# Holding back loads of x and of Q's weights behind the first statistics in a fused attention and feed-forward kernel

## The chip, the cores and the metric

One core of a Trainium2 chip. The metric is the device time of one execution in microseconds (us), the median of several. All runs here are in the fast state; the executions of one kernel can spread by 2 us and more. Two sources of that spread are found below: the grid of TensorE's clock (e5), and a pause worth 0.4 us that comes and goes.

Names: PE is TensorE (matmuls), PEld its weight loads, DVE is VectorE, ACT is ScalarE, POOL is GpSimd, SP is SyncE, which here only issues DMAs.

## The reference

```python
xn = layernorm(x)                                   # x: 2048 x 576, bf16
q, k, v = split(xn @ wqkv)                          # 32 heads of 18
pq, pk = phi(q), phi(k)                             # phi(t) = t+1 if t>0 else exp(t)
attn = ((pq @ (pk.T @ v)) / (pq @ sum(pk))) @ wo    # linear attention, per head
ffn  = (gelu(xn @ w_gate) * (xn @ w_up)) @ w_down   # 576 -> 4608 -> 576
out  = x + attn + ffn
```

## The kernel before

The part that matters is the start. x comes in 16 tiles of 128 rows. SyncE issues its loads, ScalarE's queue issues K's weights; each weight matrix is one load of 512 rows and one of 64 rows (Q's has a third, a copy of the last 64).

```python
def load_x(n0, cnt):
    nc.sync.dma_start(x_sb[:, n0:n0 + cnt, :], x_view[:, n0:n0 + cnt, :])

# ... tile pools, buffers
def load_w(which, on=nc.sync):
    c = slice(which * D, (which + 1) * D)
    on.dma_start(wqkv_sb[:, 0:4, c], A_wqkv[0:512, c].rearrange("(kt p) c -> p kt c", p=P))
    on.dma_start(wqkv_sb[0:HP, 4, c], A_wqkv[512:576, c])
    if which == 0:
        on.dma_start(wq_lo[HP:P, :], A_wqkv[512:576, c])

nc.scalar.preload_act_table_set("natural_log_exp_and_others")
load_x(0, 1)
load_x(1, 1)
load_x(2, 2)
load_x(4, 4)
load_w(0)                      # Q's weights
load_x(8, 4)
load_x(12, 4)
nc.vector.memset(wqkv_sb[HP:P, 4, :], 0.0)
nc.vector.memset(wqkv_sb[0:1, 0, D:D + 2], 0.0)
load_w(1, nc.scalar)           # K's weights
# ... identity, small constants
spin(NWARM)                    # 38 matmuls on the identity, to bring TensorE's clock up
```

Then a list `todo` of (time, step, tile), sorted by time, gives each engine its order: the statistics of a tile (`ln_stats`, DVE), its normalisation, its transposes, the K matmuls (`k_half`, two of five matmuls each), phi, and so on. Ten more warming matmuls stand in it at 5.80, 6.20 and 8.50.

```python
todo += [(t, spin, count) for t, count in [(5.80, 3), (6.20, 5), (8.50, 2)]]
todo.sort(key=lambda x: x[0])
```

Of the kernel before, what the change touches and what calls it, by code (L numbers as in the profile page):

```python
# [56 lines left out]
def kernel(  # L57
# [11 lines left out]
    nc = tc.nc  # L69
# [20 lines left out]
    x_sb = persist.tile([P, NS, D], BF16, name="x_sb")  # L90

    def load_x(n0, cnt):
        nc.sync.dma_start(x_sb[:, n0:n0 + cnt, :], x_view[:, n0:n0 + cnt, :])
# [13 lines left out]
# [6 lines that stand above are left out]
# [2 lines left out]
    load_x(0, 1)  # L115
    load_x(1, 1)
    load_x(2, 2)
    load_x(4, 4)
    load_w(0)
    load_x(8, 4)  # L120
    load_x(12, 4)

    nc.vector.memset(wqkv_sb[HP:P, 4, :], 0.0)
    nc.vector.memset(wqkv_sb[0:1, 0, D:D + 2], 0.0)
# [393 lines left out]
    def timed(steps, count):  # L518
        for step, times in steps:
            last = len(times) - 1  # L520
            for n in range(count if last >= 4 else last + 1):
                if times[min(n, last)] is not None:
                    yield times[min(n, last)] + TILE * max(n - last, 0), step, n

    todo = [*timed(STEPS, NS), *timed(Q_STEPS, NQ)]
# [6 lines left out]
        ]  # L532

    todo += [(t, spin, count) for t, count in [(5.80, 3), (6.20, 5), (8.50, 2)]]
    todo.sort(key=lambda x: x[0])

    tail = next(i for i, (_, step, n) in enumerate(todo) if step is STEPS[-1][0] and n == NS - 1) + 1
# [203 lines left out]
```

## Time and profile before

| | before |
|---|---|
| time, median (beside the changed kernel) | 527.63 us, 527.35 to 527.99 |
| span of the profiled execution | 525.2 us |
| K's large load, issued to landed | 1.95 to 9.59 us |
| TensorE's wait for it | 3.12 us |
| granted clock of TensorE over the span | 0.996 |

The time line shows the wait and the issues before it. Its columns are start, length, engine and line, operation, output and input, count, and in brackets the idle time before and what ended it.

```profile
0.81 1.82 SPq L93 DMA_DIRECT2D x_sb<-in_A_x_dram  x4
2.67 0.43 SPq L109 DMA_DIRECT2D wqkv_sb<-in_A_wqkv_dram  x1
9.63 1.36 PE L249 MATMUL ps_all<-wqkv_sb,xnT 128*128 128x288 bf16 x5 [3.12 <-DMA wqkv_sb<-in_A_wqkv_dram]
```

The reader is to see that SyncE issues four loads of x without a pause, Q's weights right behind them at 2.67, and that the first K matmuls come only at 9.63.

### The profile page before, as it was taken

To read this page: it belongs to the slowest core of one execution; us is meant where nothing else is said; L and a number is where in the kernel's file an instruction comes from. 1 tells how busy PE (TensorE), PEld (TensorE's weight loads), DVE (VectorE), ACT (ScalarE), POOL (GpSimd) and SP (SyncE) were. 2 spreads that over 40 slices of the span, in tenths; PEclk is the share of its full clock that TensorE was granted. 3 is DMA by queue.
4 is the path that set the end of the run, shared out by engine and by line. 5 is a ranking of instruction groups with operands and counts; after the bars stand their busy time and mean duration, and the time that the engine had idled before them with its cause. 6 is when DMAs were issued, how large, how long until landed. Compare 5 with 4: busy or idle time off the path is not lost.

```text
span 525.2 us, 10640 instructions
## 1 busy us (share of the span) xinstructions
PE 517.4 (99%) x4498; PEld 314.8 (60%) x4498; DVE 250.9 (48%) x435; ACT 143.2 (27%) x293; POOL 35.2 (7%) x55
## 2 busy tenths in 40 slices
PE   6999999999999999999999999999999999999997
PEld 5777764555577754444577744444777544445775
DVE  5997564987348513333378133334485233333101
ACT  3998543223230013232200023233000122322000
POOL 2021100112002100000011000000021000000000
PEclk8999999999999999999999999999999999999999
DMA  8233808899610035555400055555100355540000
GB/s 278 54 58 63 219 2 233 246 271 265 178 34 24 12 100 143 159 153 154 116 13 12 18 168 154 152 156 146 45 24 13 102 149 157 148 136 2 12 11 24
DMA packets 106282, 57.89 MB, mean 110 GB/s; under 512 B 13370, under 2 KB 105722, under 8 KB 106234
## 3 DMA queue, kind: packets, MB, share of 16 engines
q1 hardware_dynamic: 105626, 56.55, 38.3%
q8 instruction: 35, 0.57, 0.4%
q10 hardware_dynamic: 608, 0.66, 0.4%
q14 instruction: 13, 0.11, 0.1%
HBM read 52.86 MB, written 2.36 MB: 105 GB/s over the span
## 4 chain that ended last, share of the span: by engine, by line
PE 97%; DMA 2%; ACT 0%; DVE 0%; issue 0%
PE ps_all L317 55%; PE ps_all L677 27%; PE ps_all L249 4%; PE ps_all L682 4%; PE ps_all L293 4%; PE ps_all L346 2%; DMA wqkv_sb<-in_A_wqkv_dram 1%; DMA xnT<-xn 1%; PE ps_all L455 1%; PE ps_all L437 0%; PE ps_all L659 0%; ACT L114 0%; PE ps_all L235 0%; DVE res L685 0%; ACT phi_e L269 0%; PE ps_all L426 0%
## 5 line engine op out<-in xcount | busy, mean ns | idle before, releaser
L317 PE MATMUL ps_all<-xnT,wg 64*128 64x512 bf16 x1152 | 272.6, 376 | 0.0
L317 PE MATMUL ps_all<-xnT,wu 64*128 64x512 bf16 x1152 | 271.7, 376 | 0.0
L648 DVE TENSOR_TENSOR hT<-ps_all,gl 128x512 bf16<-128x512 f32 x144 | 99.5, 691 | 161.9 <-ACT gl L647 161.2
L647 ACT ACTIVATE gl<-ps_all 128x512 f32<-128x512 f32 x144 | 86.1, 598 | 314.3 <-PE ps_all L317 294.9
L317 PEld LDWEIGHTS <-wu 64*128 64x128 bf16 x1152 | 108.3, 94 | 66.3
L317 PEld LDWEIGHTS <-wg 64*128 64x128 bf16 x1152 | 108.3, 94 | 66.1
L677 PE MATMUL ps_all<-wd_sb,hT 128*128 128x288 bf16 x1152 | 147.0, 286 | 0.0
L677 PEld LDWEIGHTS <-hT 128*128 128x128 bf16 x1152 | 112.3, 98 | 30.6 <-issue 1.3
L479 DVE RECIPROCAL den_sb<-den_sb 126x128 f32<-126x128 f32 (+1 forms) x80 | 68.3, 911 | 0.5
L685 DVE TENSOR_TENSOR res<-ps_all,x_sb 128x288 bf16<-128x288 f32 x32 | 14.6, 458 | 88.0 <-PE ps_all L682 88.0
L317 PE MATMUL ps_all<-xnT,wr 64*128 64x512 bf16 x288 | 55.1, 376 | 0.0
L482 POOL TENSOR_TENSOR pqT<-pqT,den_sb 126x512 bf16<-126x512 bf16 (+3 forms) x25 | 24.2, 966 | 317.3 <-DVE den_sb L479 282.7
L249 PE MATMUL ps_all<-wqkv_sb,xnT 128*128 128x288 bf16 x160 | 23.6, 296 | 3.3 <-DMA wqkv_sb<-in_A_wqkv_dram 3.1
L682 PE MATMUL ps_all<-m_sb,pqT 126*128 126x288 bf16 (+1 forms) x160 | 24.9, 285 | 0.0
L317 PEld LDWEIGHTS <-wr 64*128 64x128 bf16 x288 | 14.5, 94 | 16.9 <-issue 0.7
L293 PE MATMUL ps_all<-hT,xn 128*128 128x288 bf16 (+4 forms) x176 | 22.4, 276 | 0.0
L249 PEld LDWEIGHTS <-xnT 128*128 128x128 bf16 x160 | 15.8, 100 | 9.6 <-issue 3.3
L293 PEld LDWEIGHTS <-xn 128*128 128x128 bf16 (+1 forms) x176 | 17.5, 101 | 4.1
L682 PEld LDWEIGHTS <-pqT 126*128 126x128 bf16 (+1 forms) x160 | 15.5, 97 | 4.1
L346 PE MATMUL ps_all<-xnT,wqkv_sb 128*126 128x512 bf16 (+1 forms) x70 | 17.4, 378 | 0.0
L277 DVE SCALAR_TENSOR_TENSOR hT<-ps_all,phi_e 128x288 bf16<-128x288 f32 x32 | 13.2, 449 | 8.1 <-ACT phi_e L273 7.5
L269 ACT ACTIVATE phi_e<-ps_all 128x288 f32<-128x288 f32 x32 | 12.9, 410 | 6.8 <-PE ps_all L249 5.5
(67 smaller groups left out, 175.3 us busy)
## 6 DMA issues: line engine op xcount, KB each, us to landing
wg<-in_B_w_gate_dram SPq DMA_DIRECT2D x72, 256.0 KB, 2.9
wu<-in_B_w_up_dram SPq DMA_DIRECT2D x72, 256.0 KB, 3.5
wd_sb<-in_B_w_down_dram SPq DMA_DIRECT2D x12, 432.0 KB, 4.5
wr<-in_B_w_gate_dram SPq DMA_DIRECT2D x72, 32.0 KB, 2.7
wr<-in_B_w_up_dram SPq DMA_DIRECT2D x72, 32.0 KB, 3.0
out_dram<-res SPq DMA_DIRECT2D x15, 144.0 KB, 1.8
x_sb<-in_A_x_dram SPq DMA_DIRECT2D x3, 576.0 KB, 8.0
wqkv_sb<-in_A_wqkv_dram SPq DMA_DIRECT2D x2, 576.0 KB, 4.5
```

The source lines that it names most:

```text
L249: nc.tensor.matmul(ps_all[:, k_bank(n, hf), :HALF], lhsT=xnT[:, kt, n * P:(n + 1) * P], rhs=wqkv_sb[:, kt, D + hf * HALF:D + (hf + 1) * HALF],
L277: nc.vector.scalar_tensor_tensor(out=out_, in0=ps, scalar=0.0, in1=e, op0=ALU.max, op1=ALU.add)
L293: nc.tensor.matmul(ps_all[:m, b, col:col + w], lhsT=xn[:, n, j0:j0 + m], rhs=pk[:, n, d0:d0 + w], start=(n == 0 and col == 0), stop=(n == ...
L317: return nc.tensor.matmul(self.outs[i], lhsT=self.lhs(i, rows, kt), rhs=self.rhs(i, rows, kt), start=start, stop=stop, skip_group_check=True,)
L346: nc.tensor.matmul(ps, lhsT=wqkv_sb[:, kt, q0:q0 + rows], rhs=xnT[:, kt, sc * SC:(sc + 1) * SC], start=(kt == 0), stop=(kt == KT - 1),)
L479: nc.vector.reciprocal(out=d[:, h:h + P], in_=d[:, h:h + P])
L482: nc.gpsimd.tensor_tensor(out=pqT[:rows, c, cols], in0=pqT[:rows, c, cols], in1=d, op=ALU.mult)
L647: nc.scalar.activation(out=gl[:], in_=ps_all[:, b[0], :], func=ACT.Gelu_apprx_tanh)
L648: nc.vector.tensor_tensor(out=hT[:, GUB * k + i, :], in0=ps_all[:, b[1], :], in1=gl[:], op=ALU.mult)
L677: nc.tensor.matmul(acc, lhsT=hT[:, f, j * P:(j + 1) * P], rhs=wd_sb[:, f, hs], start=(f == 0), stop=False,)
L682: nc.tensor.matmul(acc, lhsT=pqT[:rows, c, ts_], rhs=m_sb[:rows, c, hs], start=False, stop=(c == NCH - 1),)
L685: nc.vector.tensor_tensor(out=res[:, hs], in0=acc, in1=x_sb[:, n, hs], op=ALU.add)
```

## The change

The intent: x's tiles 4 to 15 and Q's weights aren't needed early, so they are issued only when the statistics of the first tile are done, and K's weights meet less traffic. The hold is a write of two elements into the place that the load of tile 4 will fill: the load has to wait for it, and the other loads follow in SyncE's order.

```diff
     load_x(2, 2)
-    load_x(4, 4)
-    load_w(0)
-    load_x(8, 4)
-    load_x(12, 4)
 ...
     todo += [(t, spin, count) for t, count in [(5.80, 3), (6.20, 5), (8.50, 2)]]
+
+    todo += [(4.0, lambda n: nc.vector.memset(x_sb[0:1, n, 0:2], 0.0), 4)]
+    todo += [(4.01, lambda n: load_x(n, 4), n) for n in (4,)]
+    todo += [(4.02, lambda n: load_w(0), 0)] + [(4.03, lambda n: load_x(n, 4), n) for n in (8, 12)]
```

## The prediction

> **What bounds the kernel now.** I read the page's chain first, then the waits of TensorE, then the first 16 us step by step. The chain that ended last, by engine:
>
> ```profile
> PE 97%; DMA 2%; ACT 0%; DVE 0%; issue 0%
> ```
>
> TensorE carries nearly everything. The waits of TensorE over the whole span are only three: 1.4 us at the very start, 3.1 us for a part of wqkv_sb, and 0.2 us for a transpose at 50.3 us. So the change, which touches only the first microseconds, can win at most what the 3.1 us wait holds, plus what that wait causes. The chain in order of time (start, length, what):
>
> ```profile
> 1.95 7.64 DMA wqkv_sb<-in_A_wqkv_dram
> 9.59 0.04 issue
> 9.63 1.36 PE ps_all L249 x5
> 10.99 0.53 PE ps_all L235 x5
> 11.52 1.20 PE ps_all L249 x5
> ...
> 14.96 0.28 PE ps_all L235 x5
> 15.24 0.62 PE ps_all L249 x5
> ```
>
> The load of K's weights, issued on ScalarE's queue at 1.95, lands at 9.59 and releases the first K matmuls (L249). The reader should also see that the same five matmuls take 1.36 us here and 0.62 us at 15.24, and five transposes (L235) 0.53 against 0.28. The reason is in the table of windows (stretch, its length, then busy time of PE, PEld, DVE, ACT, POOL, the granted TensorE clock, DMA share, GB/s):
>
> ```profile
> 5.79:9.20 3.41, 0.72 (x12) 0.64 (x11) 2.55 (x9) 0.98 (x3) 0.63 (x3) 1.00 1.06 353
> 9.20:12.61 3.41, 2.98 (x16) 2.10 (x16) 0.00 (x0) 1.46 (x4) 0.00 (x0) 0.50 1.05 322
> 12.62:16.00 3.38, 3.38 (x36) 2.83 (x35) 3.18 (x10) 3.32 (x12) 0.24 (x1) 1.00 0.25 98
> ```
>
> While TensorE waited (busy 0.72 of 3.41 us), the clock went to half at 9.20 and came back 3.41 us later. The clock records put the edges at 5.79, 9.20 and 12.62, on one grid of 3.413 us.
>
> Why is the load so slow? The queues in three stretches, 3.5 to 5.25, 5.25 to 7 and 7 to 9.6 us (q1 is SyncE's queue, q10 ScalarE's; packets, MB, share):
>
> ```profile
> q1 hardware_dynamic: 156, 0.42, 61.3%
> q10 hardware_dynamic: 115, 0.13, 22.7%
> ...
> q1 hardware_dynamic: 134, 0.43, 64.4%
> q10 hardware_dynamic: 203, 0.23, 37.5%
> ...
> q1 hardware_dynamic: 513, 0.58, 75.6%
> q10 hardware_dynamic: 290, 0.30, 34.7%
> ```
>
> The DMA engines are full throughout, and K's 0.66 MB get only a third of the 2.09 MB moved. The q1 bytes beside them are the end of x's tiles 2 and 3 (0.18 MB), x's tiles 4 to 7 (0.59) and most of Q's weights (0.66). For comparison, V's weights, a load of the same shape issued at 50.22 when the queues are empty, needs:
>
> ```profile
> DMA to landing us min/median/max: 4.5/4.5/4.5
> ```
>
> [...]
>
> **The change part by part.** It removes nothing from the work: the same loads with the same bytes. It adds a two-element write by VectorE into x's tile 4, after the first statistics. I compared the instruction order: it is in VectorE's stream right behind the first aggregate, and SyncE's load of tiles 4 to 7 waits for it; Q's weights and the two later x loads follow in SyncE's order. No other wait changes.
>
> - *The added write.* The aggregate runs 3.94 to 4.15 us; a small write of this kind took 0.06 us (three of them at 1.86 to 1.88). VectorE's later work moves by at most 0.1 us, and TensorE waits for weights then anyway: worth 0.
> - *The hold.* The load of tiles 4 to 7 was issued at 2.20; now at about 4.2, as SyncE starts within about 0.05 us of its release. The hold is 2 us, not until K has landed. The first x load had its first packet 1.0 us after issue, V's weights 1.2 us: so x's 4608-byte packets come from about 5.2 to 5.45 on.
> - *K before, as a check of the method.* Per DMA engine K has 36 packets, tiles 2 and 3 have 5 left at 3.85 us, tiles 4 to 7 have 8. Taking turns: 5 x (93+51) ns = 0.72, then 8 x (178+51) ns = 1.83, then 23 x (51+51) ns = 2.35; the sum ends at 8.75. It landed at 9.59[...].
> - *K after.* 5 turns with tiles 2 and 3 to 4.57; then K alone until x4 comes at 5.2 to 5.45. At 51 to 65 ns a packet that is 10 to 17 packets, in all 15 to 22. V's load, however, ramps up slowly (43 packets over all engines in its first half microsecond, 126 after one, 274 after 1.5), so I take 13 to 20. 16 to 23 remain: 8 with x (1.83 us), 8 to 15 with Q (0.8 to 1.5). End 7.85 to 8.8, plus 0.84 (0.6 if the tail shrinks with it): landing 8.4 to 9.6, centre 8.7. [...] the floor is V's time, 1.95 + 4.48 = 6.4.
> - *TensorE.* Start moves from 9.63 to about 8.75, 0.9 us. If the clock still falls at 9.20, the part before 9.20 (0.45 us) is won in full and the part from 9.20 to 9.63 (0.43 us) at half, so 0.45 + 0.2 = 0.65 us. If TensorE's load in the window is enough to keep the clock, the cold stretch is won too: its chain 9.63 to 13.12 is 3.49 us, at full clock 0.62 + 0.28 + 0.62 + 0.11 + 0.28 = 1.91, so up to 1.6 more; ScalarE, 96% busy from 11 to 16 us, would hand back part, so I count 1.0 to 1.3.
> - *Later on.* Tiles 4 to 7 are first read at 13.39, Q's weights at 16.38; their landing moves from 7.99 to about 8.5 to 9, and from 11.8 to about 12, since the total of bytes is the same and the engines stay full. Neither reaches the path. From 16 us on the chain is TensorE without gaps, so a gain at the start arrives at the end.
>
> Sum: 0.65 at the centre with the fallen clock, 2 to 3 with the clock kept or an early landing, 0 at worst; weighted about 1.1 us of 527.37, thus 526.3.
>
> **The rivals.** (1) *The hold is too short and nothing is won*: x's large packets come back while half of K is outstanding and take 78% of each turn. For it: the arithmetic above. Against: the bytes ahead of K do fall. Time 527.0 to 527.4. (2) *K really has the engines to itself and lands near 6.7*, the clock never falls: 3 us of wait plus about 1.3 of cold clock, 523.0 to 523.5. For it: V's 4.5 us alone. Against: x4 comes back at 5.3, when even V's load would have been under half done. (3) *A new wait*: tile 4's statistics or Q's first unit wait for the held loads. It would need Q's weights 2 us later than I work out; then the gain is lost and the time is 527 to 529. (4) *Clock grid*: if it shifts between executions, the runs of one kernel would spread by about a microsecond; the three of before spread by 0.5.
>
> **Range and chances.** Everything lies within 1% of 527.37, since the whole wait and the cold clock are worth 4.7 us together; 2% would be 10.5 us. Range 523.9 to 527.4. Faster by over 2%: 0.01; within: 0.98; slower: 0.01.
>
> **What would show it.** In the changed profile: SyncE's fourth load is issued at about 4.2; q10 has moved over 0.2 MB by 5.3; K's weights land between 8.4 and 9; L249's first wait is near 2.2 us; the clock still halves at 9.2 and comes back at 12.6. Wrong would be: a landing before 7.5[...], or a wait of VectorE for x.

Passages for which no trace of this case stands are cut from it: a paragraph of general rules, what the 0.84 us was put down to (it is the landing at 9.59 less the sum's end at 8.75), a clause on a possible landing at 7.5 with its cause, and the causes beside two of the signs with one of these signs. The sum came to 0.65 us at the centre, 2 to 3 in the better cases and 0 at worst, weighted about 1.1 us of 527.37, thus 526.3. That the two queues take turns packet by packet is the author's assumption in this arithmetic, not a measurement (e5 and e7 give counts for it). Measured in the packet records of before are the medians of one packet (51 ns for 1152 bytes, 93 for 2304, 178 for 4608 bytes from 4.2 to 6.5 us) and counts: from 4.2 to 6.5 us 224 of K's 1152-byte packets started, and 160 of SyncE's queue (116 of 4608 bytes, 42 of 2304, 2 of 1152). Such counts don't give the order, since the records name no engine.

## The result

| | before | after |
|---|---|---|
| time, median of 4 | 527.63 us (527.35 to 527.99) | 523.53 us (523.40 to 523.66) |
| span of the profiled execution | 525.2 us | 521.7 us |
| K's large load lands | 9.59 us | 7.37 us |
| TensorE's wait for it | 3.12 us | 0.79 us |
| first Q matmul starts | 16.52 us | 13.48 us |
| granted clock over the span | 0.996 | 1.000 |

The ratio is 0.9922, with a 95% interval of 0.9905 to 0.9939. A ratio is the mean time of one kernel's fast runs over that of the other's of the same rounds, so not quite the ratio of the medians. The gain of 4.1 us is clear of noise, and 523.53 us lies below the predicted range of 523.9 to 527.4.

The chain of the kernel after, first by engine and then in order of time (start, length, what):

```profile
PE 97%; DMA 1%; ACT 1%; DVE 0%; issue 0%
```

```profile
1.95 5.42 DMA wqkv_sb<-in_A_wqkv_dram
7.37 0.04 issue
7.41 0.79 PE ps_all L245 x5
...
8.22 0.41 ACT phi_e L265
8.63 0.58 ACT xnT L234
...
12.04 0.77 PE ps_all L245 x5
```

K's load took 5.42 us in place of 7.64. Its five matmuls (L245 is the old L249, since line numbers moved by four) took 0.79 us in place of 1.36, so the clock was full (granted 1.00 from 4.60 to 8.01, below). And between 8.2 and 12.0 the chain now runs through ScalarE and VectorE, which in the kernel before waited for a slow TensorE (its chain there is TensorE alone from 9.63 to 16 us).

The time line of the kernel after:

```profile
4.14 0.06 DVE L532 MEMSET x_sb<- 1x1 uint32 x1
4.62 0.43 SPq L109 DMA_DIRECT2D wqkv_sb<-in_A_wqkv_dram  x1
7.41 0.77 PE L245 MATMUL ps_all<-wqkv_sb,xnT 128*128 128x288 bf16 x5 [0.79 <-DMA wqkv_sb<-in_A_wqkv_dram]
```

The added write cost 0.06 us. The load of tiles 4 to 7 was issued at 4.25, 0.05 us after the write's end, Q's weights at 4.62. The queues from 3.5 to 5.25 and from 5.25 to 7 us (packets, MB, share of the 16 engines; q10 carries K):

```profile
q10 hardware_dynamic: 307, 0.35, 62.4%
q1 hardware_dynamic: 102, 0.20, 31.0%
...
q1 hardware_dynamic: 67, 0.30, 58.4%
q10 hardware_dynamic: 301, 0.31, 52.4%
```

By 5.25 us K had moved 0.35 MB, where it had moved 0.13 before. The packet records say when x came back: its first 4608-byte packet started at 5.66 us, 1.4 us after its issue, when 444 of K's 608 packets had started (queue view, 3.5 to 5.65 us; 576 of the 608 carry data). The last K packet started at 6.88.

The windows of the kernel after (stretch, length, busy PE, PEld, DVE, ACT, POOL, clock, DMA share, GB/s):

```profile
4.60:8.01 3.41, 2.29 (x28) 1.71 (x27) 3.31 (x12) 1.64 (x6) 0.48 (x2) 1.00 1.05 344
```

The clock records of this execution have their first edge at 4.60 us, where that of before had one at 5.79. On a grid of 3.41 us the window around the wait therefore is 4.60 to 8.01; TensorE was busy for 2.29 us of it, and the clock stayed at 1.00.

**Where the time went**, profile against profile, 525.2 - 521.7 = 3.5 us. The first K matmul starts 9.63 - 7.41 = 2.2 us earlier. From it to the first Q matmul it takes 13.48 - 7.41 = 6.07 us in place of 16.52 - 9.63 = 6.89, another 0.8. The last 0.4 or so lies further on: from the first Q matmul to the end of the last matmul takes 505.7 us in before and 505.3 in after. In before TensorE is released late at 50.35 us (the chain there runs through a transpose). The same 505.7 stands in e2, e8, e11 and in e16, a later run of the very kernel after, and 505.3 stands in e1, e4 and e15, so I take this part for chance, not for the change. That the medians differ by 4.1 and not 3.5 has partly to do with the clock: see e5.

### The profile page after: what moved, and what is told of

Read it like the earlier page. It is cut to its first block, busy times and chain, and to the rows that moved or that the text cites. A ratio compares the mean times of both kernels' runs of the same rounds, so it can differ in the third digit from the quotient of the medians.

```text
span 521.7 us, 10641 instructions
## 1 busy us (share of the span) xinstructions
PE 516.1 (99%) x4498; PEld 313.5 (60%) x4498; DVE 250.9 (48%) x436; ACT 143.1 (27%) x293; POOL 35.2 (7%) x55
## 4 chain that ended last, share of the span: by engine, by line
PE 97%; DMA 1%; ACT 1%; DVE 0%; issue 0%
PE ps_all L313 55%; PE ps_all L677 27%; PE ps_all L289 4%; PE ps_all L682 4%; PE ps_all L245 3%; PE ps_all L342 3%; DMA wqkv_sb<-in_A_wqkv_dram 1%; PE ps_all L451 1%; PE ps_all L433 0%; PE ps_all L659 0%; ACT xnT L234 0%; ACT L114 0%; ACT phi_e L265 0%; ACT phi_e L269 0%; DVE hT L273 0%; DVE res L685 0%
## 5 line engine op out<-in xcount | busy, mean ns | idle before, releaser
L245 PE MATMUL ps_all<-wqkv_sb,xnT 128*128 128x288 bf16 x160 | 22.5, 286 | 0.9 <-DMA wqkv_sb<-in_A_wqkv_dram 0.8
L245 PEld LDWEIGHTS <-xnT 128*128 128x128 bf16 x160 | 15.4, 98 | 6.9 <-issue 1.4
```

The costliest lines, as they stand in the source:

```text
L245: nc.tensor.matmul(ps_all[:, k_bank(n, hf), :HALF], lhsT=xnT[:, kt, n * P:(n + 1) * P], rhs=wqkv_sb[:, kt, D + hf * HALF:D + (hf + 1) * HALF],
```

## The experiments

Three questions: what of the gain is the load and what the clock; what decides when K's weights land; and is there something better still. Theory A at the start: the packets of the other queue that come between K's own. Rival B: the order in which the loads are issued. A load's lines below are from the packet records or the chain of waits of the profiled execution; times are medians. Edits are against the kernel after, if nothing else is said.

**e1: a much shorter hold.**

```diff
-    todo += [(4.0, lambda n: nc.vector.memset(x_sb[0:1, n, 0:2], 0.0), 4)]
+    todo += [(3.000, lambda n: nc.vector.memset(x_sb[0:1, n, 0:2], 0.0), 4)]   # the three loads likewise
```

> The same added write, but ahead of the first statistics, so that the held loads are issued at about 2.7 us in place of 4.2 (before: 2.2). Theory A (what keeps K's weights back is how many packets of the other queue come between its own, so each half microsecond of hold counts): K's first weights land between those of before (9.59) and after (7.37), near 8.8; time about 526 us. Rival B (any hold is enough[...]): landing near 7.4 and a time near 523.6 us.

Measured: 523.79 us (ratio to before 0.9935, 0.992 to 0.995). Tiles 4 to 7 were issued at 2.77 us, only 0.57 later than before, and this is enough. The chain and the two queues from 3.5 to 5.25 us:

```profile
1.95 5.33 DMA wqkv_sb<-in_A_wqkv_dram
```

```profile
q10 hardware_dynamic: 264, 0.30, 59.5%
q1 hardware_dynamic: 114, 0.23, 36.9%
```

K's share is nearly as good as with the long hold, and its large load landed at 7.28. x's first 4608-byte packet started at 5.85 us, 3.1 us after its issue. Theory A in its simple form falls: x was issued early and didn't come between. Something other than the hold kept it out.

**e2 and e3: longer holds**, behind the second and the third statistics (4.100 and 5.600 in place of 4.0).

> The write moved behind the second statistics, held loads issued at about 5.2 us. After, 0.35 MB + of K's 0.66 MB had moved when x came back at 5.7. Theory A: K lands at 7.0 to 7.3 (a little earlier than 7.37), TensorE's wait falls from 0.79 to about 0.5 us, time 523.2 to 523.5. Rival (the held x tiles are now late: tile 4's statistics were at 10.35 in the kernel after): a wait of VectorE for x and a time above 523.8.

> The write moved behind the third statistics, held loads issued at about 6.7 us. Theory A: K has no company at all and lands at 6.7 to 7.2, TensorE's first wait is 0.2 to 0.6 us; but x's tiles 4 to 7 land at about 10 to 10.5 and the DMA engines stand idle for about a microsecond, so the rest may come late: time 523.0 to 524.0. If Q's weights (needed at 13.3) come late as well, 524 or more.

Measured: e2 523.59 us, K's large load landed at 7.22; nothing won, nothing lost against e1's 523.79 in the same rounds. e3 524.43 us: K's large load landed at 7.49, not earlier, and x is late. Its chain:

```profile
6.96 3.87 DMA x_sb<-in_A_x_dram
...
13.19 4.94 DMA xnT<-xn
18.13 0.05 issue
18.17 1.40 PE ps_all L245 x10
```

Tiles 4 to 7 land at 10.83, the statistics and transposes of tile 4 follow, and TensorE waits 0.92 us at 18.17. This is the new wait that the prediction named as its third rival; it arises with a hold 2.7 us longer than the change's. K's large load thus needed 5.3 and 5.5 us from its issue in e2 and e3, also with hardly any company. And x's first packet came 0.96 us after its issue in both (6.12 and 7.92 us), when all or nearly all of K's packets had started. So the 1.4 us of the kernel after and the 3.1 of e1 are longer than a load needs that meets no other.

**e4: only the clock.** Against the kernel before:

```diff
-    todo += [(t, spin, count) for t, count in [(5.80, 3), (6.20, 5), (8.50, 2)]]
+    todo += [(t, spin, count) for t, count in [(5.80, 3), (6.20, 5), (6.90, 44), (8.50, 2)]]
```

> The kernel before with 44 more warming matmuls of 56 ns (2.5 us) in the 3.1 us wait for K's weights: the wait stays, only TensorE's clock is kept up. Theory C (of the 4.1 us won, about 2.2 are the earlier start and the rest the clock that no longer falls): clock 1.0 throughout, K's landing still 9.6, time 525.9 to 526.5, so a gain of 1.2 to 1.6 us. Rival (the cold stretch is hidden, ScalarE sets the pace there): under 0.5 us gained.

Measured: 525.85 us, 1.25 below the 527.10 of before in the same rounds (0.9978, 0.9958 to 0.9999, so the interval reaches almost to no gain), within the range expected. K's weights landed at 9.65, as before. The window from one edge of the clock's grid:

```profile
6.04:9.45 3.41, 3.05 (x54) 2.93 (x52) 2.45 (x9) 0.96 (x3) 0.47 (x2) 1.00 1.06 349
```

Busy all through, and the clock stays. From the first K matmul to the first Q matmul the profile takes 15.91 - 9.69 = 6.22 us in place of 6.89. So 0.7 us of the change's gain (profile) to about 1.2 (medians) can be had with idle work alone, and the other part needs the earlier load.

**e8: the kernel after without warming matmuls.**

```diff
-NWARM = 38
+NWARM = 1
-    todo += [(t, spin, count) for t, count in [(5.80, 3), (6.20, 5), (8.50, 2)]]
+    todo += [(t, spin, count) for t, count in []]
```

> The kernel after without the warming matmuls (1 in place of 38, and none of the 10 later ones): TensorE meets K's first weights with the clock at half. Theory C: the same landing of K's weights at about 7.4, but the first K matmuls take 1.3 us per five, and the time is 1.0 to 1.6 us longer than after, 524.5 to 525.1. Rival (ScalarE sets the pace in that stretch anyway): under 0.5 us longer.

Measured: 525.35 us, a little above the range expected. That is 1.8 above the 523.53 of another chip. In its profile K landed 0.44 later (7.81, a spread that the kernel after shows too, see e16) and from the first K matmul to the first Q matmul it took 14.74 - 7.86 = 6.88 us, as in the kernel before (6.89), in place of 6.07. The other 0.4 between the two profiles is the chance pause named above. The cold clock is thus worth 0.8 us of the stretch in one execution, not the 1.6 of TensorE's own work: with the fast start the chain of the kernel after runs through ScalarE from 8.2 to 11.5 us, which fits that ScalarE takes up the rest. The granted clock in the records didn't show the half pace: it reads 1.00 from 7.39 to 10.80, where five K matmuls took 1.36 us.

**e5 and e6: one of the two loads early again.** e5 issues Q's weights at 2.20 us and holds x alone; e6 issues x's tiles 4 to 7 at 2.20 and holds Q's weights.

```diff
# e5
     load_x(2, 2)
+    load_w(0)
-    todo += [(4.02, lambda n: load_w(0), 0)] + [(4.03, lambda n: load_x(n, 4), n) for n in (8, 12)]
+    todo += [(4.03, lambda n: load_x(n, 4), n) for n in (8, 12)]
# e6
     load_x(2, 2)
+    load_x(4, 4)
-    todo += [(4.0, lambda n: nc.vector.memset(x_sb[0:1, n, 0:2], 0.0), 4)]
-    todo += [(4.01, lambda n: load_x(n, 4), n) for n in (4,)]
+    todo += [(4.0, lambda n: nc.vector.memset(wqkv_sb[0:1, 0, 0:2], 0.0), 0)]
```

> Only the x loads are held; Q's weights are issued early, at 2.2 us, as 1152-byte packets beside K's 1152-byte packets. Theory A (turns packet by packet, equal packets): K gets every second packet until it is done: after tiles 2 and 3, 31 turns of 102 ns from 4.6 us, end 7.7, landing 8.2 to 8.6, time 524.3 to 525.5. Rival B[...]: landing as late as before, 9.3 or more, time 526.5 or more.

> Only Q's weights and x's tiles 8 to 15 are held, x's tiles 4 to 7 are issued early at 2.2 us (128 descriptors of 4608 bytes). Theory A: 8 turns of 229 ns beside x, then K alone: 4.6 + 1.8 = 6.4 with 13 packets done, Q's weights come at about 5.7 in the queue behind x and take every second turn from 6.4: end 8.7, landing as before, 9.2 to 9.6, and a time of 526.5 to 527.5. Rival B[...]:[...] landing near 7.5 to 8 and time near 524.

Measured: e5 527.13 us (0.9983, 0.9961 to 1.0006), K's large load at 9.50; e6 526.83 us (0.9979, 0.9958 to 1.0000), K's at 9.06. Either load alone, issued 0.25 us behind K's, takes nearly the whole gain away. e6 came in theory A's range of time (its landing a little before 9.2), and rival B, with 7.5 to 8 and 524, falls there. e5 came as rival B had it (9.3 or more, 526.5 or more): the number alone is against theory A, which expected 8.2 to 8.6. Theory A's mean was right all the same: the queues shared evenly (q10 274 packets and q1 267 between 5.25 and 7), and 524 of 576 data packets had started by 7.5 us, as the end at 7.7 requires; but the last started at 9.15. A load has landed only when all of its 16 parts are in: the semaphore of K's large load rises in 16 steps, here from 6.87 to 9.50 us, in before from 7.85 to 9.59. From 7.7 to the landing it was 1.8 us, where I had counted 0.5 to 0.9.

e5 also shows why times spread. Its four executions took 527.45, 527.45, 526.82 and 525.07 us with granted clocks of 0.994, 0.997, 0.997 and 1.000. In the profiled one the clock was low for two windows of 3.41 us, 7.95 to 14.78:

```profile
4.54:7.95 3.41, 1.72 (x24) 1.26 (x22) 3.31 (x12) 1.68 (x6) 0.47 (x2) 1.00 1.04 345
7.95:11.36 3.41, 1.82 (x11) 1.38 (x11) 0.52 (x3) 0.41 (x1) 0.24 (x1) 0.50 1.05 329
```

Half busy (1.72 of 3.41 us) was not enough to keep the clock, and half busy (1.82) was not enough to bring it back; in e6 2.27 were not enough either (7.96 to 11.37). In the other profiles, too, windows of 3.41 us with TensorE busy for 0.72 to 1.72 us were followed by the half clock (before 0.72, e9 1.27, e13 1.47, e14 1.51, e6 1.72 as e5), and those with 1.91 (e15, 4.47 to 7.88) and 2.29 (after) were not; but e7 kept the clock with 1.70, so no sharp limit shows. In the kernel before, all 34 executions of these rounds have a clock of 0.994 to 0.997, one or two low windows; with 0.994 (13 of them) they take 527.4 to 528.6 us, otherwise 526.3 to 528.0. The means differ by 0.8 us, so the clock accounts for a part of the spread. The kernel after had 0.999 or 1.000 in all nine. So the change also removes this lottery, and it fits that the medians (4.1) differ by more than two profiles (3.5), of which that of before had one low window only.

**e7: the kernel before with x's tiles 4 to 7 in small packets**, nothing held.

```diff
-    load_x(4, 4)
+    for c in (0, HALF):
+        nc.sync.dma_start(x_sb[:, 4:8, c:c + HALF], x_view[:, 4:8, c:c + HALF])
```

> The kernel before with the load of x's tiles 4 to 7 cut into two loads of 576-byte packets: the same bytes, 1024 descriptors in place of 128, nothing held. Theory A: K's turns beside x cost about 51 + 30 ns in place of 229, so K lands at 7.7 to 8.3 and the time falls to 524 to 525.5, while tile 4 lands later. Rival B[...]: K lands later than before, 9.6 or more, time 527.5 or more.

Measured: 525.38 us (0.9957, 0.9939 to 0.9975), K's large load at 8.59 in place of 9.59 (its small one only at 9.37, needed by each fifth matmul). Same bytes, eight times the packets, and K is faster. From 4.5 to 7.0 us 454 packets of K and 478 of x's 576-byte ones started, nearly one for one, which is 0.52 MB of K beside 0.28 of x. In before, in the same stretch, it was 281 of K's and 120 of x's 4608-byte ones, 0.32 MB beside 0.55. Here theory A holds in direction (it expected 7.7 to 8.3), and rival B, which expected 9.6 or more, falls.

**e9: is K's small load what keeps x out?** From e1: K's 64-row load is taken from ScalarE's queue and issued on SyncE's, behind x's tiles 4 to 7. D stands for yes: x, now second in order, should share with K's large load. E stands for no: x should wait as in e1.

```diff
-        on.dma_start(wqkv_sb[0:HP, 4, c], A_wqkv[512:576, c])
+        if which != 1:
+            on.dma_start(wqkv_sb[0:HP, 4, c], A_wqkv[512:576, c])
+    todo += [(3.0015, lambda n: nc.sync.dma_start(wqkv_sb[0:HP, 4, D:2 * D], A_wqkv[512:576, D:2 * D]), 0)]
```

> The kernel of the early hold (held loads issued at 2.77 us), but K's second, small load (64 rows) taken from ScalarE's queue and issued on SyncE's behind x's tiles 4 to 7. Theory D[...]: now x stands second, its 4608-byte packets come at about 3.8 to 4.3 us and K's large load lands at 9 or later, time 526 to 527.5. Rival E[...]: x's first packet at 5.6 to 5.9 and K's large load at 7.2 to 7.5 as in the early hold, time 523.5 to 524.3.

Measured: 525.53 us. x's first packet at 5.54 us, as rival E has it, so theory D falls. K's large load nevertheless landed at 8.75, not at 7.2 to 7.5: 492 of its 512 packets had started by 6.5 us, and the last 20 dragged on to 7.87 between x's large ones. This tail sits in a few of the load's 16 parts: 13 semaphore steps had come by 6.70 us, the last three at 7.29, 8.60 and 8.75. It was not expected and I don't explain it; the time can't be held against either theory.

**e10: no hold at all, only another order.** Against the kernel before:

```diff
-    load_x(2, 2)
+    load_x(2, 1)
+    load_x(3, 1)
```

> The kernel before, nothing held, no added write; only the load of x's tiles 2 and 3 cut into two, so that SyncE issues tiles 4 to 7 at about 2.65 us in place of 2.20, after K's small load (2.42). If the place in the order is all that counts (D or E), K lands at 7.2 to 7.6, x's 4608-byte packets begin at 5.6 or later, the clock stays full and the time is 523.4 to 524. Theory A (bytes ahead of K): the same bytes are issued, only 0.45 us later, so K lands at 9.2 or later and the time is 526.5 or more.

Measured: 524.90 us (0.9952, 0.9936 to 0.9967), 2.65 below before, with no added write and no wait of SyncE for VectorE. Tiles 4 to 7 are now issued at 2.67 us, and their first packet came at 6.22; the load of tile 3 (2.19) shared with K instead, and K's large load landed at 7.70, its small one at 8.68, for which the fifth matmul waited another 0.33 us:

```profile
2.41 6.27 DMA wqkv_sb<-in_A_wqkv_dram
8.68 0.04 issue
8.72 0.30 PE ps_all L250
```

Theory A (526.5 or more) falls; D and E (523.4 to 524) were 0.9 too low, since they forgot the load that now stands in x's old place.

**e13: where is the limit?** From e1, with the write between two halves of an earlier clearing.

```diff
-    nc.vector.memset(pqT[HP:P, NCH - 1, 0:2 * SC], 0.0)
+    nc.vector.memset(pqT[HP:P, NCH - 1, 0:SC], 0.0)
+    nc.vector.memset(x_sb[0:1, 4, 0:2], 0.0)
+    nc.vector.memset(pqT[HP:P, NCH - 1, SC:2 * SC], 0.0)
```

> The early hold, with the added write between two halves of an earlier clearing, so that tiles 4 to 7 are issued at about 2.4 to 2.5 us: 0.45 to 0.55 us behind K's large load (1.95). Measured so far: x issued 0.25 us behind K's large load shares with it (before, first packet 4.17), x issued 0.82 us behind it waits (early hold, first packet 5.85). Theory E with a limit between 0.25 and 0.38 us (in the kernel with the sooner K, a load 0.38 us behind it waited): first packet of x at 5.5 or later, K's large load at 7.2 to 7.6, time 523.3 to 524.3. Rival (the limit lies at the issue of K's second load, or in how long the hold is): x's first packet at 4.2 to 4.6, K at 8.8 or later, time 525.5 or more.

Measured: 528.10 us (1.0004, 0.9987 to 1.0022): no gain. x was issued at 2.43 us, and the chain and the queues from 3.5 to 5.25 read:

```profile
1.95 8.36 DMA wqkv_sb<-in_A_wqkv_dram
```

```profile
q1 hardware_dynamic: 135, 0.29, 63.7%
q10 hardware_dynamic: 116, 0.13, 30.9%
```

Compare with e1: 0.34 us of difference in the issue of the held loads, 0.13 MB in place of 0.30 for K, and a ratio to before of 1.0004 in place of 0.9935, which is 3.6 us. x's first packet came at 4.36. My limit of 0.25 to 0.38 us was wrong, and all three of the rival's numbers came (4.2 to 4.6, 8.8 or later, 525.5 or more). Its reading that K's small load sets the limit has e9 and e12 against it: in e9 the small load is issued behind x, in e12 at 1.82, behind the load of tiles 2 and 3 at 1.73, and x waited in both. Here x issued 0.48 us behind K's large load still shares, 0.72 (e10) and 0.82 (e1) don't. The limit isn't one fixed time, though: in e12 below, where K's load is issued at 1.35, a load 0.38 us behind it had its first packet only at 4.31, 2.6 us after its issue.

**e14: K's large load in two halves**, otherwise e1. E1: x waits for the first half alone, E2: for both.

```diff
-        on.dma_start(wqkv_sb[:, 0:4, c], A_wqkv[0:512, c].rearrange("(kt p) c -> p kt c", p=P))
+        for k0 in (0, 2) if which == 1 else (0,):
+            k1 = k0 + 2 if which == 1 else 4
+            on.dma_start(wqkv_sb[:, k0:k1, c], A_wqkv[k0 * P:k1 * P, c].rearrange("(kt p) c -> p kt c", p=P))
```

> The early hold (x issued at 2.77 us) with K's large load cut into two of half the rows, issued at 1.95 and about 2.4. Theory E1[...]: x's first packet at 4.6 to 5.1, and K's second half lands at 8 or later, time 524.5 to 526.5. Rival E2[...]: x's first packet at 5.5 or later, K's second half at 7.2 to 7.6, time 523.3 to 524.3.

Measured: 527.09 us, with executions from 524.46 to 529.28. x's first packet at 5.51 and K's halves landed at 6.24 and 7.02, about as E2 has it: x waited for both. But E2's time of 523.3 to 524.3 was missed: K's small load, now third on ScalarE's queue, was issued at 2.93, 0.16 us behind x, and there the order turned:

```profile
2.93 6.32 DMA wqkv_sb<-in_A_wqkv_dram
9.29 0.40 PE ps_all L247
```

It landed 6.32 us later, at 9.25, behind x's four tiles (8.89), though its own queue held nothing else once K's halves were in at 7.02, and TensorE waited 1.82 us for it; in e1 it had landed at 7.64. So here the load issued second came second, on whichever queue. That is no general rule: loads issued 0.24 to 0.48 us behind K's (before, e5, e6, e10's tile 3, e13) shared with it.

**e11, e12, e15, e16: is there something better?** In the kernel after, ScalarE leads from 8.2 to 11.5. e11 moves one of its copies to VectorE, e12 lets K's weights start sooner, e15 puts e11's copy on e1, and e16 is the kernel after once more, as the reference on e15's chip. The second case of e12's expectation is that x's tiles 1 to 3 land later, with K issued sooner.

```diff
# e11; e15 is the same with e1's shorter hold
-        (tp_copy, [x_, 7.98, 9.53, 11.92]),
+        (lambda n: tp_copy(n, copy=vcopy if n == 1 else acopy), [x_, 8.07, 9.53, 11.92]),
# e12
-    nc.vector.memset(wqkv_sb[HP:P, 4, :], 0.0)
+    nc.vector.memset(wqkv_sb[HP:P, 4, D:2 * D], 0.0)
     nc.vector.memset(wqkv_sb[0:1, 0, D:D + 2], 0.0)
     load_w(1, nc.scalar)
+    nc.vector.memset(wqkv_sb[HP:P, 4, 0:D], 0.0)
+    nc.vector.memset(wqkv_sb[HP:P, 4, 2 * D:3 * D], 0.0)
```

> The kernel after with one copy of the second tile's transposes (0.69 us) moved from ScalarE to VectorE, which stood idle then. In the kernel after ScalarE carries the chain from 8.2 to 11.5 us. If it sets the pace there: TensorE's first Q matmul comes 0.3 to 0.7 us earlier than 13.48, time 522.8 to 523.3. If TensorE or VectorE takes its place at once: 523.4 to 523.8.

> The kernel after with VectorE's clearing of wqkv_sb cut so that only K's third stands before K's load: it is issued at about 1.4 us in place of 1.95. If the chain K's load to first K matmul still leads: K lands 0.3 to 0.5 us earlier, time 522.9 to 523.3. If [...] the first transposes or the statistics of tile 2 come late, and the time is 523.6 to 524.5.

> The early hold together with the copy moved to VectorE. In the kernel after with the copy moved, TensorE's first Q matmul came 5.85 us after K's first matmul in place of 6.07, and the time was 523.21. If the early hold costs nothing against the longer one: 522.9 to 523.4, and 0.2 to 0.5 us below the kernel after of the same rounds. If x's earlier packets slow K's last ones: above that.

> The kernel after, unchanged, as the reference of the same chip and rounds for the run with the moved copy: 523.3 to 523.8. If it is no slower than the run with the moved copy (within 0.1 us), the moved copy is not shown to win anything.

Measured: e11 523.21 us (0.9919, 0.9907 to 0.9931; within 522.8 to 523.3), e15 523.42 (523.19 to 523.61), e16 523.74 (523.40 to 524.26), e12 524.08 (within 523.6 to 524.5, for x's tiles come late). In e15's chain TensorE goes on without ScalarE between:

```profile
7.74 0.78 PE ps_all L245 x5
8.51 0.28 PE ps_all L231 x5
8.79 0.61 PE ps_all L245 x5
...
11.93 0.76 PE ps_all L245 x5
```

From the first K matmul to the first Q matmul it took 13.36 - 7.74 = 5.62 us in e15 against 13.86 - 7.80 = 6.06 in e16. That part is clear. The medians differ by 0.3 us with overlapping runs, so a total gain is likely but not established; e15 also differs from e16 in its hold. In e11's profile K's load happened to land at 6.67, so its first Q matmul at 12.56 owes 0.7 us to that and 0.2 to the copy. In e12 K's large load landed at 6.01, but x's tiles 2 and 3, issued 0.38 us behind it, landed at 6.96 in place of 5.64; their statistics came late and TensorE waited 0.98 us at 8.26: one load's place is another's delay. e16's profile has K landing at 7.75 where the first profile of the same kernel has 7.37; with e8 and e11, whose loads are the same, the spread is 6.67 to 7.81, so the landings under different holds (7.22 to 7.49 in e1 to e3) can't be told apart.

## Why the prediction was wrong

*What bounds the kernel, and that the whole change lies in the first 16 us*: right. Every gain at the start arrived at the end. *The added write*: right, 0.06 us, off the path. *The hold of 2 us and the issue at about 4.2*: right, 4.25.

*"K after"*: this is the step that failed. It said: "then K alone until x4 comes at 5.2 to 5.45", with 13 to 20 of 36 packets per engine done by then, and a landing at 8.7 (the middle of its own range, 8.4 to 9.6, would have been 9.0). Measured: x's first packet at 5.66, and by 5.5 us 391 of K's 576 data packets had started, 24 per engine; the landing was 7.37. Two terms were mis-sized in the same direction. K alone was quicker than V's load, whose slow beginning I had applied to it (in half microseconds from each load's first packet 65, 140, 146 packets, against V's 38, 79, 141); in e16, the same kernel, it was as slow as V's (23, 84, 128). The return took 1.4 us in place of 1.0 to 1.2, and 1.8 in e16 (4.26 to 6.06), where K landed at 7.75 in spite of its slow start: so the return is the term that counts. The tail, 0.5 us from the last packet's start to the landing, can't be set beside the 0.84 of the prediction: that was counted from the end of a sum over 36 packets, the small load's four included, to the landing of the large load alone (the small one landed at 10.22). The rule behind the step, that x's return is its issue plus about a microsecond, is what the runs overturn: in e1 x was issued at 2.77 and came at 5.85, while in e2 and e3, with K nearly through, it came after 0.96. What the runs put in its place is a condition on the order of issue (with K's load issued at 1.95, x shared up to 0.48 us behind it, e13, and waited from 0.72 us on, e10), not a length of hold. Why there is such a condition stays open (below).

*"TensorE"*: the mechanism was right, the choice was not. I took the fallen clock as the centre and the kept one as the better case. The clock was kept, since the wait was 0.79 us and not 2.2. The worth of the cold stretch, 1.0 to 1.3 us after ScalarE's part, was about right to somewhat high: 0.7 to 0.8 in the stretch (e4, e8, and before against after) and 1.25 in the time (e4, with an interval of 0.05 to 2.2).

*The grid*: I argued that a moving grid would spread the runs by a microsecond, and that they spread by 0.5. The grid does move (the first edge on record is at 4.60 us in the first profile of the kernel after, at 5.60 in e16), and the runs do spread: over 34 executions of before from 526.3 to 528.6 us, on four chips and by 1.4 to 2.0 on each. Three runs were too few to say.

*The rivals*: the second one, "K really has the engines to itself", with 523.0 to 523.5 us, is what happened within 0.1 us. That its number fits is partly luck: it had K landing near 6.7 (7.37) and 3 us of wait won (2.3), and a part of the gain comes from what it didn't name, such as the pause of 0.4 us in the profile of before. The stated range began at 523.9 and left this rival out. It was dismissed with "x4 comes back at 5.3, when even V's load would have been under half done". The first rival (nothing won) describes e13; the third (x late) describes e3. Of the signs named, the moved 0.2 MB by 5.3 came out (0.35), the landing between 8.4 and 9, the wait near 2.2 and the halving at 9.2 did not, and the sign set down for a wrong prediction, a landing before 7.5, was there.

**What stays open.** Why one load waits and another shares isn't shown. The records of the issues don't settle it: in e13 that of K's large load had ended at 2.39, before x's began at 2.43, and the two shared all the same. Measured is the order alone: x's tiles 4 to 7, issued 0.72 us (e10) and 0.82 us (e1, and the same hold in e9 and e14) behind K's first load, had their first packet at 6.22, 5.85, 5.54 and 5.51, while loads issued 0.25 to 0.48 us behind K's (before, e5, e6, e13) shared with it. e12's limit, the tail of e9 and the spread of landings of one set of loads (6.67 to 7.81) aren't explained either.

## What to carry to other kernels

When a load on the critical path shares the DMA engines, look at which loads are issued just before and just behind it, on all queues: a shift of 0.3 us in the issue of the held loads was worth 3.6 us here (e13 against e1), and a hold longer than needed only moved the wait elsewhere (e3: 0.92 us at 18.17). Judge a wait of TensorE together with the clock that it costs (0.7 to 0.8 us of the stretch here, e4 and e8), and test the two apart with idle matmuls. K's large load landed when the last of its 16 parts was in, later than its mean share of the engines said: 1.8 us later in e5, and in the kernel after 0.5 us after its last packet had started. So allow for such a tail.
